# Start slices of the last three pieces of w_out: 28, 36 and 44 for pieces 5, 6 and 7, where only pieces 6 and 7 had start slices, 34 and 44

## The chip, the cores and the metric

The kernel runs on one core of one Trainium2 chip. The metric is the device time of one execution in microseconds (us). Before the change the median of three runs is 434.64 us (432.01 to 434.95).

## What is computed

Three layers follow one another. The first is a decayed linear attention over 2 x 768 tokens with 8 heads of 64. The second, which is where the change lies, projects to 1024 channels, takes the positive part, convolves three neighbouring tokens, gates with a sigmoid and projects back to 512. The third routes each token to one of eight experts and applies that expert's two matrices.

```python
h = np.maximum(x @ w_in, 0.0)                 # 512 -> 1024
conv_out += conv_w[k] * hp[:, k:k + S, :]     # k = 0, 1, 2
gate = 1.0 / (1.0 + np.exp(-conv_out))
x2 = (h * gate) @ w_out                       # 1024 -> 512
logits = x2 @ w_gate; e = argmax(logits)      # with a local gate that may keep the last expert
out = p[e] * (relu(x2 @ w1[e]) @ w2[e])
```

## The kernel before, in words

The inputs w_in and w_out arrive as 64-bit words that hold a float32 each, split over two 32-bit halves. A piece is 128 x 512 numbers. `convert` (line 160) turns one piece into a pair of float32r tiles (high and low part), which the matmuls use as three products (`mm3`, line 131: lines 133, 134, 135). There are 8 pieces of w_in and then 8 of w_out, numbered m = 0 to 7 here.

The steps of `convert` for a piece of w_out are: DMA of the words into `raw` (line 143); `narrow`, which on DVE shifts and merges the high words into `na` (lines 149, 150), on ACT scales the low words in place (line 151) and on POOL adds the two (line 153); then ACT writes the high part `woh` (line 174), DVE the low part `wol` (line 176); PE transposes the piece into `wt_ps` (line 185), ACT copies it out to `wt` (line 189), PE multiplies it by the router's weights into `wc_ps` (line 193), and ACT copies the 9 columns to `wc` (line 195). A `yield n` in these generators says after how many ticks of `advance` (line 404) the next step is issued; so the steps of a piece are spread over the program between other work.

The same engines at the same time run the middle layer for batch 0. `ffn_in` (line 366) takes a block of 128 channels (m = 0 to 7) in 8 slices of 3 matmuls each (`h_ps`, 128 x 384, two halves of the tokens, four slices for each half); ACT takes the positive part (line 376). When a block's slices are over, `hidden` (line 346) follows behind the next block at the ticks of TIMES (line 380): ACT scales by the first tap (line 350), DVE adds the other two (line 353 twice), ACT takes the sigmoid (line 355), DVE multiplies (line 357), ACT cuts off the high part (line 326), DVE the low part (line 330), and PE forms the router's logits `lg` (line 344). So in a block's round of 8 slices each engine has its `hidden` steps at fixed places.

The program is scheduled by hand: each engine executes its instructions in the order in which this Python code issues them. An instruction whose input is late holds everything behind it on its engine. PSUM tiles come from pools: `h_ps` and `wc_ps` share the three buffers of `psa` (line 457) once the attention is over, `wt_ps` has the two of `psg` (line 458). From then on the loop of line 461 issues one slice of `ffn_in` and one `advance` in turn, and `slices[0]` counts the slices.

What sets where a piece begins is the waiting loops ahead of its `narrow`: not more than two other pieces may hold buffers (line 167), and, for pieces named in GATES (line 157), the slice counter must have reached the number given there (line 169).

Of the kernel before, what the change touches and what calls it, by code (L numbers as in the profile page):

```python
# [91 lines left out]
def tile_kernel(ctx, tc, cat, cst, qT, kT, kN, vN, w_in, conv_w, w_out, wg, w1, w2, out):  # L92
# [61 lines left out]
        yield 2  # L154
        return a.bitcast(F32)

    GATES, slices = {6: 34, 7: 44}, [0]
    turning, held, loaded, ready, banks = [], [], [], [], [0]

    def convert(src, hi, lo, m=None):  # L160
# [902 lines left out]
```

## Time and profile before

| what | value |
|---|---|
| median of three runs | 434.64 us (432.01 to 434.95) |
| the profiled execution | 432.95 us, its span 431.2 us |
| PE busy | 408.8 us, 95% of the span |
| DVE, ACT, POOL busy | 289.6, 259.2 and 91.5 us |
| mean granted clock | 0.99 of full speed |

Times in the views are counted from the start of the span. A line of a timeline gives the start, the duration, the engine, the line of the kernel, the operation, the tile written and the tiles read, and in brackets how long the engine was idle before it and what ended that. PE is the matmul engine, and its weight loads, named PEld, run beside it. In the span the middle layer's slices of batch 0 run from about 55 to 135 us, and the attention before and beside them until about 90 us.

### The profile page before, as it was taken

To read this page: it belongs to the slowest core of one execution; us is meant where nothing else is said; L and a number is where in the kernel's file an instruction comes from. 1 tells how busy PE (TensorE), PEld (TensorE's weight loads), DVE (VectorE), ACT (ScalarE), POOL (GpSimd) and SP (SyncE) were. 2 spreads that over 40 slices of the span, in tenths; PEclk is the share of its full clock that TensorE was granted. 3 is DMA by queue.
4 is the path that set the end of the run, shared out by engine and by line. 5 is a ranking of instruction groups with operands and counts; after the bars stand their busy time and mean duration, and the time that the engine had idled before them with its cause. 6 is when DMAs were issued, how large, how long until landed. Compare 5 with 4: busy or idle time off the path is not lost.

```text
span 431.2 us, 7291 instructions
## 1 busy us (share of the span) xinstructions
PE 408.8 (95%) x2412; PEld 329.2 (76%) x2412; DVE 289.6 (67%) x518; ACT 259.2 (60%) x429; POOL 91.5 (21%) x92
## 2 busy tenths in 40 slices
PE   8898999999899999999999999999999999999991
PEld 7787897899798778988768776867738677776880
DVE  3798789787767260377899058968664796858650
ACT  2787677667666212566704166869556686958560
POOL 5256664211110000000000330305203132211210
PEclk9999999999899999999999999999999999999997
DMA  7989763230000101000197899999969999774100
GB/s 229 388 291 398 260 211 92 93 97 1 2 0 2 49 26 49 26 0 2 58 377 254 304 373 379 342 390 409 398 254 340 407 364 346 280 260 186 44 25 29
DMA packets 27324, 86.59 MB, mean 201 GB/s; under 512 B 3598, under 2 KB 4622, under 8 KB 27280
## 3 DMA queue, kind: packets, MB, share of 16 engines
q1 hardware_dynamic: 25200, 79.76, 50.4%
q0 software_dynamic: 2080, 6.29, 3.9%
q8 instruction: 21, 0.34, 0.3%
q14 instruction: 23, 0.19, 0.1%
HBM read 105.18 MB, written 6.55 MB: 259 GB/s over the span
## 4 chain that ended last, share of the span: by engine, by line
PE 35%; issue 26%; DMA 15%; DVE 14%; ACT 4%; POOL 3%; SPq 1%; POOLq 0%; DVEq 0%; ACTq 0%
DMA out_dram<-yo,it 13%; PE h_ps L133 5%; PE h_ps L134 4%; PE h_ps L135 4%; PE x_ps L133 4%; PE x_ps L134 3%; PE x_ps L135 3%; PE y L300 3%; DVE cc L353 3%; PE s_ps L282 2%; POOL xg L727 2%; PE inc L290 1%; DMA kq<-in_qT_dram 1%; PE y L302 1%; DVE na L149 1%
## 5 line engine op out<-in xcount | busy, mean ns | idle before, releaser
L133 PE MATMUL h_ps<-xT,wih 128*128 128x384 f32 x128 | 46.9, 366 | 0.0
L353 DVE SCALAR_TENSOR_TENSOR cc<-h,cw,cc 128x768 f32<-128x768 f32 x32 | 34.4, 1075 | 18.6 <-ACT cc L350 18.5
L863 POOL DMA_INDIRECT out_dram<-yo,it x13 | 16.7, 1282 | 136.3 <-ACT yo L862 136.3
L727 POOL DMA_INDIRECT xg<-xs,it x13 | 18.8, 1444 | 123.4 <-DMA qc<-in_w_dram 115.8
L134 PE MATMUL h_ps<-xT,wih 128*128 128x384 f32 x128 | 43.5, 340 | 0.0
L135 PE MATMUL h_ps<-xT,wil 128*128 128x384 f32 x128 | 43.4, 339 | 0.0
L133 PE MATMUL x_ps<-woh,hg 128*128 128x512 f32 x96 | 38.5, 401 | 0.0
L134 PE MATMUL x_ps<-wol,hg 128*128 128x512 f32 x96 | 37.6, 391 | 0.0
L135 PE MATMUL x_ps<-woh,hg 128*128 128x512 f32 x96 | 37.5, 391 | 0.0
L718 DVE TENSOR_TENSOR ws0l<-r,ws0l 128x1024 fp32r<-128x1024 f32 x22 | 26.0, 1221 | 16.3 <-ACT ws0l L717 16.2
L153 POOL TENSOR_TENSOR na<-na,raw 128x512 int32<-128x512 int32 (+1 forms) x17 | 21.9, 1289 | 48.9 <-ACT raw L151 17.7
L300 PE MATMUL y<-at,vz 128*128 128x128 f32 x192 | 30.6, 281 | 1.8 <-ACT vz L277 0.9
L718 DVE TENSOR_TENSOR ws0h<-r,ws0h 128x1024 fp32r<-128x1024 f32 x22 | 26.0, 1221 | 8.2 <-ACT ws0h L717 8.2
L718 DVE TENSOR_TENSOR wc<-r,wc 128x1024 fp32r<-128x1024 f32 x22 | 25.9, 1221 | 8.0 <-ACT wc L717 8.0
L717 ACT ACTIVATE ws0l<-r 128x1024 fp32r<-128x1024 f32 x22 | 22.1, 1052 | 13.9 <-PE y L135 13.9
L282 PE MATMUL s_ps<-qz,kq 128*128 128x256 f32 x96 | 29.2, 386 | 1.0 <-issue 1.0
L718 DVE TENSOR_TENSOR ws1h<-r,ws1h 128x1024 fp32r<-128x1024 f32 x22 | 26.0, 1221 | 6.0 <-ACT ws1h L717 3.8
L717 ACT ACTIVATE wc<-r 128x1024 fp32r<-128x1024 f32 x22 | 22.1, 1054 | 11.3 <-PE g L135 11.3
L300 PEld LDWEIGHTS y<-at,vz 128*128 128x128 f32 x192 | 25.4, 191 | 4.3 <-DVE xT L305 2.3
L284 DVE TENSOR_TENSOR at<-s_ps,ca 128x256 f32<-128x256 f32 x48 | 20.2, 420 | 11.7 <-PE s_ps L282 11.6
L133 PEld LDWEIGHTS h_ps<-xT,wih 128*128 128x128 f32 x128 | 24.6, 192 | 3.1 <-issue 1.8
L489 ACT ACTIVATE xn<-x_ps 128x512 f32<-128x512 f32 x10 | 6.0, 599 | 32.8 <-PE x_ps L135 18.2
(231 smaller groups left out, 1044.9 us busy)
## 6 DMA issues: line engine op xcount, KB each, us to landing
r<-in_w_dram SPq DMA_DIRECT2D x88, 512.0 KB
qc<-in_w_dram SPq DMA_DIRECT2D x32, 512.0 KB
qs1l<-in_w_dram SPq DMA_DIRECT2D x32, 512.0 KB
raw<-in_w_in_dram SPq DMA_DIRECT2D x8, 512.0 KB
raw<-in_w_out_dram SPq DMA_DIRECT2D x8, 512.0 KB
kq<-in_qT_dram SPq DMA_DIRECT2D x7, 384.0 KB
kq<-in_kT_dram SPq DMA_DIRECT2D x7, 384.0 KB
kv<-in_vN_dram SPq DMA_DIRECT2D x7, 384.0 KB
```

What stands on the lines that cost most here:

```text
L133: te.matmul(ps, lhi, rhi, start=first, stop=False)
L134: te.matmul(ps, lhi, rlo, start=False, stop=False)
L135: te.matmul(ps, llo, rhi, start=False, stop=last)
L153: po.tensor_tensor(out=a, in0=a, in1=lo, op=ALU.add)
L282: te.matmul(ps, self.kq[:, 0, tok], self.qz[:, :, tok], start=True, stop=True)
L284: ve.tensor_tensor(out=self.at[c], in0=ps, in1=self.dm, op=ALU.mult)
L300: te.matmul(y, vz[:, c, j, :], at[:, j, :], start=(j == 0), stop=(c == 0 and j == 1))
L353: ve.scalar_tensor_tensor(out=cc, in0=h[:, i:i + S], scalar=cw[:, m, i:i + 1], in1=cc, op0=ALU.mult, op1=ALU.add)
L717: se.activation(out=w[:, 0, h, :], in_=r, func=AF.Copy)
L718: ve.tensor_tensor(out=w[:, 1, h, :], in0=r, in1=w[:, 0, h, :].bitcast(F32), op=ALU.subtract)
L727: return po.indirect_dma_start(out=xg, out_offset=None, in_=xs[0:n], in_offset=bass.IndirectOffsetOnAxis(ap=it[:, j:j + 1], axis=0), bound ...
L863: po.indirect_dma_start(out=out, out_offset=bass.IndirectOffsetOnAxis(ap=it[:, j:j + 1], axis=0), in_=yo, in_offset=None, bounds_check=NT ...
```

## The change

GATES gets an entry for piece 5 and a later one for piece 6. Blocks have 8 slices, so 28, 36 and 44 are the same place (the middle) in the rounds of three blocks in a row.

```diff
-    GATES, slices = {6: 34, 7: 44}, [0]
+    GATES, slices = {5: 28, 6: 36, 7: 44}, [0]
```

No instruction is added or taken away. PE, DVE and ACT get another order in about three rounds; SP (which issues the loads) and POOL keep theirs. In the rows below a number behind a name tells buffers apart (na_1196 before and na_1232 after are both piece 5, na_1295 and na_1306 piece 6, na_1373 piece 7; cc_1285 before and cc_1279 after are the same block's channels, and so are cc_1218 and cc_1214). A semaphore that the instruction waits for stands in brackets.

ACT, in the first round after slice 28, before:

```order
L195 ACTIVATE wc_96<-wc_ps_1248 128x9 [waits PE_49]
L376 ACTIVATE h0_131<-h_ps_1238 128x384 [waits PE_49]
L195 ACTIVATE wc_96<-wc_ps_1257 128x9
L350 ACTIVATE cc_1285<-h0_131,cw_93 128x768 [waits Activation_49]
L189 ACTIVATE wt_1287<-wt_ps_1262 128x512
L189 ACTIVATE wt_1293<-wt_ps_1276 128x512 [waits PE_49]
L151 ACTIVATE raw_1134<-raw_1134 128x512 [waits DMAHW1_49]
L376 ACTIVATE h1_132<-h_ps_1281 128x384 [waits PE_49]
L326 ACTIVATE hg_1307<-cc_1218 128x768 [waits DVE_49]
L355 ACTIVATE cc_1285<-cc_1285 128x768 [waits DVE_49]
```

ACT at the same place, now:

```order
L195 ACTIVATE wc_96<-wc_ps_1245 128x9 [waits PE_49]
L376 ACTIVATE h0_131<-h_ps_1236 128x384 [waits PE_49]
L195 ACTIVATE wc_96<-wc_ps_1255 128x9
L174 ACTIVATE woh_102<-na_1232 128x512 [waits Pool_49]
L350 ACTIVATE cc_1279<-h0_131,cw_93 128x768 [waits Activation_49]
L189 ACTIVATE wt_1281<-wt_ps_1260 128x512
L376 ACTIVATE h1_132<-h_ps_1275 128x384 [waits PE_49]
L326 ACTIVATE hg_1301<-cc_1214 128x768 [waits DVE_49]
L189 ACTIVATE wt_1304<-wt_ps_1288 128x512
L151 ACTIVATE raw_1134<-raw_1134 128x512 [waits DMAHW1_49]
```

The scaling of the next block (line 350, cc_1285 and cc_1279) stood straight behind two small copies; now the high part of piece 5 (line 174, na_1232), which waits for POOL, stands ahead of it. Before, that instruction (as na_1196) stood seven rows ahead of line 350.

DVE in the same round, before:

```order
L353 SCALAR_TENSOR_TENSOR cc_1218<-h2_133,cw_93,cc_1218 128x768 [waits DVE_49]
L176 TENSOR_TENSOR wol_103<-na_1196,woh_102 128x512 [waits Activation_49]
L330 TENSOR_TENSOR hg_1235<-cc_1108,hg_1235 128x768 [waits Activation_49]
L353 SCALAR_TENSOR_TENSOR cc_1285<-h0_131,cw_93,cc_1285 128x768 [waits PE_49,Activation_49]
L149 TENSOR_SCALAR na_1295<-raw_1134 128x512 [waits DMAHW1_49,PE_49]
L150 SCALAR_TENSOR_TENSOR na_1295<-raw_1134,na_1295 128x512 [waits DVE_49]
L357 TENSOR_TENSOR cc_1218<-cc_1218,h2_133 128x768
```

and now:

```order
L353 SCALAR_TENSOR_TENSOR cc_1214<-h2_133,cw_93,cc_1214 128x768 [waits DVE_49]
L149 TENSOR_SCALAR na_1232<-raw_1083 128x512 [waits DMAHW0_49,PE_49]
L150 SCALAR_TENSOR_TENSOR na_1232<-raw_1083,na_1232 128x512 [waits DVE_49]
L330 TENSOR_TENSOR hg_1229<-cc_1108,hg_1229 128x768 [waits Activation_49]
L353 SCALAR_TENSOR_TENSOR cc_1279<-h0_131,cw_93,cc_1279 128x768 [waits PE_49,Activation_49]
L176 TENSOR_TENSOR wol_103<-na_1232,woh_102 128x512 [waits Pool_49]
```

The two `narrow` steps of a piece (lines 149, 150) stood behind the first tap of the next block (line 353); now they stand ahead of it and ahead of line 330. Those of piece 5 had stood four rows above the first one shown. The same pattern follows one round later with piece 6; piece 7 keeps its two rows where they were.

PE in the round of piece 7 (block after slice 44), before:

```order
L133 MATMUL h_ps_1399<-xT_159,wih_100 128x384
L134 MATMUL h_ps_1399<-xT_159,wih_100 128x384
L135 MATMUL h_ps_1399<-xT_159,wil_101 128x384
L193 MATMUL wc_ps_1409<-wgs_92,wt_1364 128x9 [waits Activation_49]
L193 MATMUL wc_ps_1409<-wgs_92,wt_1364 128x9 x3
L185 MATMUL wt_ps_1415<-cs_91,na_1373 128x128 [waits Pool_49]
L185 MATMUL wt_ps_1415<-cs_91,na_1373 128x128 x3
L133 MATMUL h_ps_1399<-xT_197,wih_100 128x384
```

and now:

```order
L133 MATMUL h_ps_1399<-xT_159,wih_100 128x384
L134 MATMUL h_ps_1399<-xT_159,wih_100 128x384
L135 MATMUL h_ps_1399<-xT_159,wil_101 128x384
L185 MATMUL wt_ps_1410<-cs_91,na_1373 128x128 [waits Pool_49]
L185 MATMUL wt_ps_1410<-cs_91,na_1373 128x128 x3
L133 MATMUL h_ps_1399<-xT_197,wih_100 128x384
L134 MATMUL h_ps_1399<-xT_197,wih_100 128x384
L135 MATMUL h_ps_1399<-xT_197,wil_101 128x384
L193 MATMUL wc_ps_1419<-wgs_92,wt_1371 128x9 [waits Activation_49]
L193 MATMUL wc_ps_1419<-wgs_92,wt_1371 128x9 x3
```

The transposes of piece 7 (line 185), which wait for POOL, stood behind the router product of piece 6 (line 193); now they stand ahead of it, with three matmuls between. The rounds of pieces 5 and 6 have their transposes at the same place, after the first half's second slice.

## Rows read from the trace of the kernel before

**Rows 1.** Page, parts 1 and 2: busy us (share), and PE's granted clock
```profile
PE 408.8 (95%) x2412; PEld 329.2 (76%) x2412; DVE 289.6 (67%) x518; ACT 259.2 (60%) x429; POOL 91.5 (21%) x92
PEclk9999999999899999999999999999999999999997
```
**Rows 2.** Waits of PE, 60 to 250 us: total, times, longest
```profile
PE wc_ps L193 <- ACT h L376: 1.6, 1, 1.6
PE pb L621 <- DVE pi L558: 0.8, 1, 0.8
```
**Rows 3.** Windows: us, then busy us (instructions) by engine, PEclk, DMA share, GB/s
```profile
110.00:111.00 1.00, 0.00 (x0) 0.00 (x0) 0.55 (x1) 1.00 (x3) 0.00 (x0) 1.00 0.00 0
...
114.00:115.00 1.00, 1.00 (x5) 1.00 (x4) 1.00 (x2) 0.44 (x1) 0.00 (x0) 0.50 0.00 0
```
**Rows 4.** Timeline of PE, 100 to 123 us
```profile
100.52 0.95 PE L193 MATMUL wc_ps<-wgs,wt 128*128 128x9 f32 x8
101.33 0.63 PE L185 MATMUL wt_ps<-cs,na 128*128 128x128 f32 x4
101.72 0.42 PE L133 MATMUL h_ps<-xT,wih 128*128 128x384 f32 x1
...
103.42 0.44 PE L133 MATMUL h_ps<-xT,wih 128*128 128x384 f32 x1
...
109.60 0.34 PE L135 MATMUL h_ps<-xT,wil 128*128 128x384 f32 x1
111.50 1.35 PE L193 MATMUL wc_ps<-wgs,wt 128*128 128x9 f32 x8 [1.57 <-ACT h L376]
...
113.46 0.67 PE L133 MATMUL h_ps<-xT,wih 128*128 128x384 f32 x1
...
116.06 0.34 PE L133 MATMUL h_ps<-xT,wih 128*128 128x384 f32 x1
...
122.19 0.34 PE L133 MATMUL h_ps<-xT,wih 128*128 128x384 f32 x1
```
**Rows 5.** Timeline of POOL, 90 to 120 us
```profile
97.63 1.32 POOL L153 TENSOR_TENSOR na<-na,raw 128x512 int32<-128x512 int32 x1 [4.62 <-ACT wt L189]
107.09 1.76 POOL L153 TENSOR_TENSOR na<-na,raw 128x512 int32<-128x512 int32 x1 [8.13 <-DVE na L150]
```
**Rows 6.** Timeline of DVE, 95 to 132 us
```profile
102.34 0.69 DVE L176 TENSOR_TENSOR wol<-na,woh 128x512 fp32r<-128x512 f32 x1
102.94 0.95 DVE L330 TENSOR_TENSOR hg<-cc,hg 128x768 fp32r<-128x768 f32 x1
104.75 1.02 DVE L353 SCALAR_TENSOR_TENSOR cc<-h,cw,cc 128x768 f32<-128x768 f32 x1 [0.86 <-ACT cc L350]
105.69 0.42 DVE L149 TENSOR_SCALAR na<-raw 128x512 int32<-128x512 int32 x1
106.14 0.69 DVE L150 SCALAR_TENSOR_TENSOR na<-raw,na 128x512 int32<-128x512 int32 x1
106.75 0.95 DVE L357 TENSOR_TENSOR cc<-cc,h 128x768 f32<-128x768 f32 x1
107.62 2.05 DVE L353 SCALAR_TENSOR_TENSOR cc<-h,cw,cc 128x768 f32<-128x768 f32 x1
```
**Rows 7.** Timeline of ACT, 95 to 132 us
```profile
95.61 0.59 ACT L189 ACTIVATE wt<-wt_ps 128x512 f32<-128x512 f32 x1
...
98.03 0.94 ACT L350 ACTIVATE cc<-h,cw 128x768 f32<-128x768 f32 x1
98.99 0.63 ACT L174 ACTIVATE woh<-na 128x512 fp32r<-128x512 f32 x1
...
103.21 0.16 ACT L195 ACTIVATE wc<-wc_ps 128x9 f32<-128x9 f32 x1
103.26 0.48 ACT L376 ACTIVATE h<-h_ps 128x384 f32<-128x384 f32 x1
...
103.78 0.94 ACT L350 ACTIVATE cc<-h,cw 128x768 f32<-128x768 f32 x1
...
120.21 0.92 ACT L350 ACTIVATE cc<-h,cw 128x768 f32<-128x768 f32 x1
```

## The prediction

> **What bounds the kernel now.** The page first: PE is busy for 95% of the span, and its granted clock is at full speed (2.4 GHz) but for one slice of the forty and the tail [rows 1]. So PE sets the pace, and time is won or lost where PE stands still or runs slowly. The waits of PE from 60 to 250 us come next: the longest is 1.6 us, a router product of line 193 that waits for ACT's line 376; the second is half as long [rows 2]. The windows place it: from 110 to 111 us PE does nothing, and from 114 to 115 us the granted clock is 0.50, which is 1.2 GHz [rows 3]. PE had been busy up to the hole, the hole came first, and the low clock followed.
>
> The timeline of PE prices that place [rows 4]. The last matmul ahead of the hole starts at 109.60; the next would have followed after 0.17 us (twelve matmuls of 128 x 384 take 2.06 us start to start), at 109.77, and starts at 111.50: 1.73 us lost. At full clock a router product and the transposes behind it last 101.72 - 100.52 = 1.20 us; here they last 113.46 - 111.50 = 1.96 us. The nine matmuls behind them last 116.06 - 113.46 = 2.60 us against 9 x 0.172 = 1.55 us. The clock costs 0.76 + 1.05 = 1.81 us, the whole place 3.5 us. That is 0.8% of the time and the most that a better place for the pieces can win here; from 116.06 to 122.19 PE runs without a hole to speak of.
>
> Why ACT was late is in the timelines of DVE and POOL. POOL's addition for piece 6 (line 153) runs from 107.09 to 108.85 [rows 5]; it takes 1.76 us where the one for piece 5 took 1.32. DVE's line 353, issued at 107.62, takes 2.05 us where the same instruction took 1.02 at 104.75 [rows 6]. Each held the other: the addition waited for line 357, which ended at 107.70, and line 353 waited for the addition. From 107.70 to 108.85 is 1.15 us: an addition ends 1.15 us after the DVE instruction that held it.
>
> **What the change does, step by step.** No instruction comes or goes, and SP's and POOL's order stays, so no load moves past another in a queue. Three pieces get the same place in three rounds. I walk the new order with durations of before; an instruction of ACT or DVE that waits for nothing starts about 0.08 us before its predecessor's recorded end [rows 6].
>
> Round one. ACT's copy at 95.61 is common to both orders [rows 7]. Line 151 of piece 5 no longer stands behind it, so the next block's line 350 starts at 95.61 + 0.49 + 0.39 + 0.49 + 0.53 = 97.51 instead of 98.03: ACT's steps for line 189, line 376, line 189 again and line 174, start to start. The early part gains 0.5 us. DVE follows: line 353 at 97.51 + 0.97 = 98.48, then line 176 (+0.94), 357 (+0.60), 353 (+0.87), 149 (+0.94), 150 (+0.45), which gives 102.28, and line 330 (+0.61) at 102.89, to 103.84. Line 150 ends at 102.97, and POOL would start 0.26 us later (106.83 to 107.09 in [rows 5, 6]); but line 330 is then running, as line 357 was in [rows 6], so the addition ends at 103.84 + 1.15 = 104.99. ACT meanwhile reaches the row that the change put ahead of line 350: line 174, which needs that sum. ACT is there at 103.7 (before, line 350 started there, at 103.78 [rows 7]) and waits 1.3 us. PE starts the block at 103.29 instead of 103.42 (the copy of line 195, which frees its buffer, ends at 103.24 by the walk and ended at 103.37 [rows 7]); its six matmuls last 6 x 0.172 + 0.12 = 1.15 us, it reaches the transposes at 104.44, and they wait for the sum: 0.6 us of hole, up to 105.05.
>
> From here it is a ring, the same in all three rounds: line 174 on ACT, line 350, then DVE's 353, 176, 357, 353, 149, 150 and 330, POOL's addition held until 330 ends, and line 174 of the next piece. Its length, start to start: 0.53 + 0.97 + 0.94 + 0.60 + 0.87 + 0.94 + 0.45 + 0.61 + 0.95 + 1.15 + 0.04 = 8.05 us, from [rows 6, 7] and the 1.15 above. PE's own work between two sets of transposes is one block: 24 matmuls at 0.172, logits 0.46, router product 0.81, transposes 0.39, and 0.65 of starts behind changes of shape: 6.44 us. So PE stands still for 8.05 - 6.44 = 1.6 us in each round. The second set of transposes starts at 105.05 + 8.05 = 113.10, the third at 121.15. Behind the third come three matmuls (0.39 + 0.64 us), the router product (0.81) and three more (0.63): the next block starts at 121.15 + 2.47 = 123.6. In the trace of before it starts at 122.19 [rows 4]. **The sum is +1.4 us.** It holds the hole and the low clock of before, which go, and three new holes (0.6, 1.6 and 1.6 us), which come.
>
> What is late next: ACT's line 350 of the following block, at about 121.7 against 120.21 [rows 7]. No piece is left in the rounds behind it, DVE and ACT get by on less than PE's 5.8 us for each, and the logits still find their input ready, by half a microsecond. The lag of PE stays and is carried to the end, since PE's later waits are 0.8 us at most up to 250 us [rows 2].
>
> The profiled execution took 432.95 us (span 431.2 and 1.75 around it), so the sum gives 434.4 on its own base. The three timed runs have a median 1.7 us higher, and what is forecast is a median: 434.64 + 1.4 = 436.0 us.
>
> One price has two bounds: whether line 330 holds POOL. The rows show line 357 holding it (1.76 against 1.32 us, [rows 5]), and both are the same operation, with both inputs in SBUF. If 330 does not hold it, the addition ends 0.26 + 1.28 after line 150, at 104.5, and the ring is 0.49 us shorter: three rounds give 1.4 us back and the sum is zero. I take the held value, because the row nearest to it is the same operation on the same engine.
> The Trainium skill has two pages on this. "Advanced Engine Details and Errata", section "VectorE Performance Modes", names only Vector instructions in a two-port mode as blocking GpSimd, and gives tensor_tensor no such mode; by it the sum would be zero. "SBUF — State Buffer", section "Who interferes with whom", says that a Vector instruction with two inputs in SBUF contends with a GpSimd instruction that reads SBUF, and that the first to issue holds the other for its whole length; by it the sum is +1.4. This case's trace agrees with the second, with its 1.76 us addition and its 2.05 us line 353.
>
> **The rivals.** (1) The third hole lowers the clock as the hole of before did (1.73 us there, 1.6 here). A fall behind the second hole costs 1.8 us too, but the third hole takes 1.6 of it; one behind the third is paid in full: 1.4 + 1.8 = +3.2, 437.8 us. For it speaks the equal size, against it that a hole of 0.6 us and PE's many short gaps lowered nothing. (2) Line 330 does not hold POOL: 434.6 us, as worked out. (3) Faster: evenly spaced pieces never meet the stream, the hole of 109.77 goes and nothing comes for it: 434.64 - 3.5 = 431.1 us. It needs a ring of no more than 6.44 us, or the sum ready when ACT reaches line 174, 1.3 us earlier than the walk has it; that line 330 stands between line 150 and the addition speaks against it. (4) Slower: the clock stays at 1.2 GHz from the second hole to the end of the third round. PE's 6.44 + 2.47 = 8.9 us of work would take 2.60 / 1.55 = 1.68 times as long, 15.0 us from 113.1: the next block starts at 128.1, 5.9 us later than before, 440.5 us. It decides from some 11 us of low clock on, since each costs 0.4 us and the third hole absorbs 1.6; before, the clock was low for about 4 us.
>
> **How the numbers follow.** Sum as worked out, with or without a low clock that the third hole absorbs: 0.53. Rival 1: 0.23. Rival 2: 0.10. Rival 3: 0.07. Rival 4: 0.07. The predicted time is 436.0 us. The range leaves out rivals 3 and 4 (0.14): below it takes rival 2 less half the spread of the runs shown (434.6 - 1.5 = 433.1), above rival 1 with 0.8 us for its clock, 438.6. About 1% of the time, 4.3 us, is what a measurement of this kernel can tell from no change. Faster by more than that would need more than the 3.5 us that the place holds: 0.03. Slower by more than that is rival 4 with a little of rival 1: 0.09. Within 1%: 0.88.
>
> **What would show it.** Line 350 of the three rounds in the timeline of ACT, 8 us apart (about 97.5, 105.6, 113.7, 121.7), each straight behind a line 174 that waited for POOL; PE's transposes of line 185 waiting for POOL three times, 0.6, 1.6 and 1.6 us; additions of about 1.8 us; the block behind the third set at about 123.6 us. The hole at 109.8 us gone, with its wait for line 376. Wrong would be: additions of 1.3 us (rival 2), line 350 less than 7 us apart and no wait at line 185 (rival 3), or a granted clock of 0.5 in the stretch around 121 to 125 us (rival 1) or throughout from 113 us on (rival 4).

## The result, and the profile after

The changed kernel takes 436.93 us in the median of 11 runs (435.09 to 438.70), the kernel before 434.64 us in 11 runs beside it. The ratio is 1.0053, with a 95% interval of 1.0028 to 1.0078, which is 2.3 us more, from 1.2 to 3.4. The forecast was 436.0 us, a sum of +1.4.

| what | before | after |
|---|---|---|
| median | 434.64 us | 436.93 us |
| profiled execution, its span | 432.95, 431.2 us | 436.16, 434.4 us |
| mean granted clock of that execution | 0.990 | 0.988 |
| PE's waits for POOL at line 185, 60 to 250 us | none among those listed | 3.4 us in 3 |
| PE's wait for line 376 at line 193 | 1.6 us | none |

The page of the changed kernel, the row of PE in part 1 and the granted clock in part 2, answers [rows 1]:

```profile
PE 407.4 (94%) x2412; PEld 328.0 (76%) x2412; DVE 288.2 (66%) x518; ACT 258.8 (60%) x429; POOL 92.2 (21%) x92
PEclk9999999999999999999999899999999999999996
```

The low slice of before, the eleventh (108 to 119 us), is full now. Another has fallen in its stead, the twenty-third, at about 245 us. The waits of PE from 60 to 250 us (total, times, longest) answer [rows 2]:

```profile
PE wt_ps L185 <- POOL na L153: 3.4, 3, 1.6
PE tp L813 <- DMA xg<-xs,it: 2.3, 1, 2.3
```

The hole at line 193 is gone and three at line 185 have come, all behind POOL's additions. The second row, a transpose of gathered tokens far behind the change, was 0.8 us before. The timeline of ACT (start, duration, line, tiles, idle time ahead) shows the instruction that makes the ring:

```profile
104.35 0.63 ACT L174 ACTIVATE woh<-na 128x512 fp32r<-128x512 f32 x1 [1.37 <-POOL na L153]
104.89 0.92 ACT L350 ACTIVATE cc<-h,cw 128x768 f32<-128x768 f32 x1
...
112.36 0.63 ACT L174 ACTIVATE woh<-na 128x512 fp32r<-128x512 f32 x1 [0.97 <-POOL na L153]
112.90 0.92 ACT L350 ACTIVATE cc<-h,cw 128x768 f32<-128x768 f32 x1
...
120.37 0.63 ACT L174 ACTIVATE woh<-na 128x512 fp32r<-128x512 f32 x1 [0.92 <-POOL na L153]
120.91 0.92 ACT L350 ACTIVATE cc<-h,cw 128x768 f32<-128x768 f32 x1
```

Three times line 350 stands straight behind a line 174 that waited for POOL, 8.01 us apart. The timelines of DVE and POOL show the link from line 330 to the addition (the first round):

```profile
102.21 0.95 DVE L330 TENSOR_TENSOR hg<-cc,hg 128x768 fp32r<-128x768 f32 x1
105.84 1.02 DVE L353 SCALAR_TENSOR_TENSOR cc<-h,cw,cc 128x768 f32<-128x768 f32 x1 [2.68 <-ACT cc L350]
```
```profile
102.55 1.77 POOL L153 TENSOR_TENSOR na<-na,raw 128x512 int32<-128x512 int32 x1 [10.16 <-ACT wc L195]
110.58 1.75 POOL L153 TENSOR_TENSOR na<-na,raw 128x512 int32<-128x512 int32 x1 [6.26 <-DVE na L150]
118.56 1.77 POOL L153 TENSOR_TENSOR na<-na,raw 128x512 int32<-128x512 int32 x1 [6.24 <-ACT raw L151]
```

The addition ends at 104.32, 1.16 us after line 330 (103.16), and lasts 1.77 us. DVE then stands idle for 2.68 us because line 350 is late, and that delay comes back to POOL one round later. And the timeline of PE, the end of the third round, for the block whose start was forecast:

```profile
120.39 0.66 PE L185 MATMUL wt_ps<-cs,na 128*128 128x128 f32 x4 [1.61 <-POOL na L153]
...
122.83 0.34 PE L133 MATMUL h_ps<-xT,wih 128*128 128x384 f32 x1
```

That block starts 0.64 us later than at 122.19 in [rows 4], although this execution left the attention 0.63 us earlier: its first logits (line 344) start at 94.76, those of before at 95.39. Over the rounds it lost 1.27 us.

For the comparisons below, **the stretch** is the time on PE from the first line-344 group after 94 us to the sixth: 34.71 us before (95.39 to 130.10) and 35.99 us after (94.76 to 130.75). The difference of 1.28 us is made up as follows. Before holds a hole of 1.57 and a low clock of 1.81. After holds holes of 0.27, 0.46, 0.18, 1.33 and 1.61, together 3.85. That leaves 31.33 against 32.14 us, or 0.8 us for the same instructions. In the new order three matmuls stand between line 185 and line 193 in each round, so PE changes shape more often; that this is what costs was read from the order and not tried by itself. Most of the remainder is not the holes' doing: the first experiment, with one hole of 0.28 us and the same three matmuls between, keeps 32.12 - 0.28 = 31.84 us, 0.5 us more than before.

### The profile page after: what moved, and what is told of

The parts are those of the page before. It is cut to its first block, busy times and chain, and to the rows that moved or that the text cites. A ratio compares the mean times of both kernels' runs of the same rounds, so it can differ in the third digit from the quotient of the medians.

```text
span 434.4 us, 7289 instructions
## 1 busy us (share of the span) xinstructions
PE 407.4 (94%) x2412; PEld 328.0 (76%) x2412; DVE 288.2 (66%) x518; ACT 258.8 (60%) x429; POOL 92.2 (21%) x92
## 4 chain that ended last, share of the span: by engine, by line
PE 32%; issue 27%; DMA 17%; DVE 14%; ACT 4%; POOL 3%; SPq 1%; POOLq 0%; DVEq 0%; ACTq 0%
DMA out_dram<-yo,it 15%; PE h_ps L133 4%; PE x_ps L133 4%; PE h_ps L134 4%; PE h_ps L135 4%; PE x_ps L134 3%; PE x_ps L135 3%; PE y L300 3%; DVE cc L353 3%; PE s_ps L282 2%; DMA kv<-in_kN_dram 2%; PE inc L290 1%; DVE na L150 1%; DVE cc L357 1%; PE y L302 1%
## 5 line engine op out<-in xcount | busy, mean ns | idle before, releaser
L353 DVE SCALAR_TENSOR_TENSOR cc<-h,cw,cc 128x768 f32<-128x768 f32 x32 | 33.3, 1042 | 23.0 <-ACT cc L350 22.9
L489 ACT ACTIVATE xn<-x_ps 128x512 f32<-128x512 f32 x10 | 6.0, 599 | 32.8 <-PE x_ps L135 15.5
```

What stands on the lines that cost most here:

```text
L353: ve.scalar_tensor_tensor(out=cc, in0=h[:, i:i + S], scalar=cw[:, m, i:i + 1], in1=cc, op0=ALU.mult, op1=ALU.add)
```

## The experiments

**One step later, the ring is open.** The edit puts a tick of delay between the narrowing of a late piece and its line 174. That instruction then stands behind line 350 on ACT and no longer ahead of it; what follows in the piece (line 176 on DVE, the transposes of line 185 on PE) comes a tick later too.

```diff
         w = yield from narrow(words, 512)
+        if m in GATES: yield 1
```

> Edit on the changed kernel: pieces of w_out issue line 174 and all their steps behind it one tick later, so that ACT's line 350 stands ahead of line 174. Ring theory (ACT waits at line 174 for POOL's sum, which waits for line 330, and line 350 stands behind it, 8.05 us a round): the ring is open, line 350 comes about 6.4 us after its predecessor (DVE's own rounds with one held addition), the three waits of line 185 for POOL go, the place of the three rounds gets some 4 us shorter: about 431.5 us, ratio to before 0.990 to 0.995. Rival A (the time is lost at the gather behind the second layer, where PE waited 2.3 us for line 727 in the changed kernel against 0.8 before, because the later rounds shift it against the loads): the rounds get shorter but the time stays near 436 us. Rival B (DVE and POOL together are the bound of a round, whatever the order on ACT): line 350 stays 7.5 to 8 us apart, 435 to 437 us.

Measured: 430.84 us against 434.07 us for before, ratio 0.991 (0.9877 to 0.9943). ACT's timeline and the window from 110 to 130 us (busy time of PE, PEld, DVE, ACT, POOL, then the clock):

```profile
109.40 0.94 ACT L350 ACTIVATE cc<-h,cw 128x768 f32<-128x768 f32 x1
110.77 0.63 ACT L174 ACTIVATE woh<-na 128x512 fp32r<-128x512 f32 x1 [0.36 <-POOL na L153]
115.80 0.94 ACT L350 ACTIVATE cc<-h,cw 128x768 f32<-128x768 f32 x1
```
```profile
110.00:130.00 20.00, 20.00 (x140) 17.89 (x139) 15.51 (x20) 13.95 (x25) 3.04 (x3) 1.00 0.00 1
```

Line 350 comes every 6.15 to 6.40 us, PE is busy for all 20 us, and the stretch is 32.12 us. The slices are the same 28, 36 and 44, and the additions are as long as in the changed kernel (1.78, 1.81 and 1.78 us). So neither the place in the round nor the held addition costs the time by itself: the wait of line 174 ahead of line 350 sets the 8 us. The transposes, which are no link of that ring, now stand behind nine matmuls of the block and not six, and start 0.06 us after each sum is ready (the additions end at 104.40, 110.73 and 117.05, the transposes start at 104.46, 110.79 and 117.11). How much of the three holes went by this later place, and how much by the shorter round, was not parted. The time is 3.2 us below before, where rival 3 priced 3.5. This version beats both kernels.

**Two slices later.** The same opening without an added step (against the changed kernel):

```diff
-    GATES, slices = {5: 28, 6: 36, 7: 44}, [0]
+    GATES, slices = {5: 30, 6: 38, 7: 46}, [0]
```

> Edit on the changed kernel: GATES = {5: 30, 6: 38, 7: 46}, the same place in each round again, but two slices later; line 174 then stands behind line 350 on ACT and lines 149 and 150 behind line 330 on DVE, with no other edit. Ring theory: what costs is that line 174 stands ahead of line 350 and the transposes ahead of the sum, not that the pieces have the same place: the ring is open, lines 350 about 6.4 us apart, no wait of line 185 for POOL, the stretch of logits near 32.2 us, time as with the extra tick, about 431 us, ratio 0.990 to 0.995. Rival (three pieces in three consecutive rounds are too dense for DVE and POOL wherever they stand): lines 350 7.5 to 8 us apart, ratio 1.000 to 1.005.

Measured: 431.49 against 433.72 us, ratio 0.9957 (0.9931 to 0.9982). Line 350 comes 6.33, 6.61 and 6.78 us apart, PE's waits at line 185 are 0.5 us in two, and the stretch is 32.80, all a little more than expected (ratio 0.990 to 0.995, 32.2 us). Here POOL issues first, and then it is DVE that is held (POOL's timeline, then DVE's):

```profile
103.62 1.31 POOL L153 TENSOR_TENSOR na<-na,raw 128x512 int32<-128x512 int32 x1 [11.11 <-DVE na L150]
```
```profile
104.25 1.50 DVE L353 SCALAR_TENSOR_TENSOR cc<-h,cw,cc 128x768 f32<-128x768 f32 x1 [0.88 <-ACT cc L350]
```

**One slice earlier** ({5: 27, 6: 35, 7: 43} in the same line).

> Edit on the changed kernel: GATES = {5: 27, 6: 35, 7: 43}, the same place in each round, one slice earlier. Line 174 still stands ahead of line 350 on ACT, but lines 149 and 150 now stand ahead of DVE's second line 353 instead of behind it. Ring theory: the ring stays closed but is shorter: line 350 to 353 0.97, then 0.94, 0.87 (line 357), 0.45, 0.61, line 353 held against the addition 1.01, addition 1.15, 0.04, line 174 0.53, line 376 0.39: 6.96 us a round against 8.05. Lines 350 come 7.0 us apart, the stretch from the first to the sixth group of logits is about 3 us shorter than the 36.0 of the changed kernel, 432 to 433.5 us, ratio to before 0.995 to 0.999: between the changed kernel and the two with the ring open. Rival (only the order of lines 174 and 350 counts, so a closed ring costs what it cost in the changed kernel): lines 350 8 us apart, ratio 1.005.

Measured: 432.34 against 435.49 us, ratio 0.9947 (0.9914 to 0.9979), a little better than expected. Line 350 is 7.68, 7.09 and 7.08 us apart against an expected ring of 6.96, the additions are held (1.82 to 1.85 us), PE waits 0.8 us in two at line 185 and 0.96 us once for line 195, the clock does not fall, and the stretch is 33.77 (about 33 was expected). ACT's timeline shows that line 174 still waits ahead of line 350:

```profile
110.83 0.63 ACT L174 ACTIVATE woh<-na 128x512 fp32r<-128x512 f32 x1 [0.31 <-POOL na L153]
111.37 0.47 ACT L376 ACTIVATE h<-h_ps 128x384 f32<-128x384 f32 x1
111.87 0.94 ACT L350 ACTIVATE cc<-h,cw 128x768 f32<-128x768 f32 x1
```

The ring is shorter, and so are the holes.

**The held addition by itself.** The ticks of lines 326 and 330 are moved in three blocks (11 and 13 become 13 and 14), so that line 330 comes later and POOL goes first; the slices stay those of the change.

```diff
-    LATE = {(B - 1, 5): ...
+    LATE = {**{(0, m): (0, 1, 3, 4, 10, 13, 14, 15) for m in (1, 2, 3)}, (B - 1, 5): ...
```

> Edit on the changed kernel: for blocks 1 to 3 of batch 0 line 326 goes from tick 11 to 13 and line 330 from 13 to 14, so that line 330 becomes ready only after POOL's addition has begun. Ring theory with line 330 as a link: the additions last 1.3 us instead of 1.76, the ring is 0.49 us shorter (7.55 us between lines 350), the third transposes come 1.5 us earlier: about 1.5 us less than the changed kernel, ratio to before about 1.001. Rival (the addition is slow for another reason, such as ACT's or PE's traffic): additions stay at 1.76 us, line 350 stays 8.0 us apart, time as the changed kernel, ratio about 1.005.

Measured: 432.77 against 434.07 us, ratio 0.9974 (0.9946 to 1.0001). POOL's and ACT's timelines:

```profile
111.82 1.28 POOL L153 TENSOR_TENSOR na<-na,raw 128x512 int32<-128x512 int32 x1 [6.27 <-DVE na L150]
119.34 1.28 POOL L153 TENSOR_TENSOR na<-na,raw 128x512 int32<-128x512 int32 x1 [6.24 <-DVE na L150]
```
```profile
106.12 0.92 ACT L350 ACTIVATE cc<-h,cw 128x768 f32<-128x768 f32 x1
...
113.14 0.63 ACT L174 ACTIVATE woh<-na 128x512 fp32r<-128x512 f32 x1 [0.65 <-POOL na L153]
113.67 0.92 ACT L350 ACTIVATE cc<-h,cw 128x768 f32<-128x768 f32 x1
```

The ring still closes (line 174 waits ahead of line 350), but a round is 7.52 to 7.59 us, not 8.01: that is the 0.49 us by which the prediction shortened it without the hold. The stretch is 34.55 us, 1.4 less than the changed kernel's, as rival 2 worked out for three rounds. The time is a miss: the expected ratio of about 1.001 lies outside the interval, and the median is some 1.6 us lower than expected. The ring accounts for the 1.4 us only. The mean granted clock of these twelve executions is higher too (median 0.9925 against 0.987), but whether that is the rest is not shown.

**One piece of the change at a time.** First piece 5 alone ({5: 28, 6: 34, 7: 44}), then piece 6 alone ({6: 36, 7: 44}).

> One part alone: GATES = {5: 28, 6: 34, 7: 44}, so only piece 5 is moved. Ring theory by the walk: round one as in the changed kernel (line 350 1.7 us later than before, a hole of 0.6 us at line 185), then piece 6 meets the stream as before, with line 353 held by the addition, and PE waits for line 376 again, some 2 us: 1.7 us slower than before, ratio 1.004. Rival (the moves add up evenly, 1.15 us of the measured 2.3 each): ratio 1.0026.

> One part alone: GATES = {6: 36, 7: 44}, so only piece 6 is moved and piece 5 begins as early as before. Ring theory by the walk: round one as before without piece 6 in it (line 350 at 103.8), rounds two and three 8.05 us each, holes of 1.0 and 1.6 us at line 185, the hole before line 193 gone: the block behind the third transposes starts at 121.9 against 122.2 before, 0.3 us faster than before without a low clock, ratio 0.999. Rival (the moves add up evenly): ratio 1.0026.

Piece 5 alone: 434.04 us, ratio 0.9975 (0.9944 to 1.0007). That is a miss: 1.004 lies outside. The stretch is 35.07 us, 0.4 over the 34.71. The walk had kept the hole of before at line 193 and its low clock behind the new hole; the trace has no low clock there and only a rest of the hole. PE itself was later (among others 1.3 us in a wait of line 344 for line 357); line 376 ends at 113.36 us, and line 193 starts at 113.42, some 0.3 us later than it could. Piece 6 alone: 434.04 us, ratio 0.9997 (0.9963 to 1.0031), the time as expected, but with one wait of 2.1 us at line 185 where two of 1.0 and 1.6 were worked out, and a stretch of 33.68 us. The prices of the two pieces, +0.4 and -1.0 us in the stretch, don't add up to the +1.28 of both. Each version alone already has a round of the ring's length (8.06 us between lines 350 with piece 5, 8.02 with piece 6), and each takes away the hole and the low clock of before, 3.4 us that can be won only once. How the rest divides was not tried.

**The same kernels once more.** A single pair of profiles can't tell how often the clock falls, so before and the changed kernel were each profiled again, unchanged.

> The kernel before, unchanged, profiled once more. The walk's sum took the low clock behind the hole of line 193 (1.81 us) as part of before. Theory C (a hole of this size lowers the clock in some executions and not in others): the hole of 1.5 to 1.8 us ahead of line 193 is there again with the same wait for line 376, and the granted clock behind it may stay at 1.00; then the stretch from the first to the sixth group of logits behind 95 us (34.7 us in the first profile) takes 33.0 us. Rival (the hole always lowers it): 34.7 us again, granted clock near 0.5 for some 3 us behind the hole.

> As the run ahead of it, a third profile of the kernel before: 33.0 us or 34.7 us between the first and the sixth group of logits behind 95 us, by whether the granted clock falls behind the hole.

> The changed kernel, unchanged, profiled once more. Ring theory: lines 350 8.0 us apart again, three waits of line 185 for POOL. Theory C: the clock may fall behind one of the holes; if it falls behind the third, the stretch between the first and the sixth group of logits takes 36.0 + 1.8 = 37.8 us, otherwise 36.0 to 36.4 us. The wait of line 813 for the gather at about 245 us, 2.3 us in the first profile of after and 0.8 in that of before, comes out anywhere between 0.7 and 3 us if it has nothing to do with the change, and at 2 us or more if the change causes it.

> The changed kernel, profiled a third time, for two terms that the walk left to chance. Clock: it fell behind a hole in three of three profiles of before and in one of two of the changed kernel; the stretch of logits is 36.0 us without a fall and 37.3 us or more with one. Gather: if the change makes the wait of line 813 longer, it is 1.0 us or more again (0.5 to 0.8 in three profiles of before); if not, it is 0.5 to 0.8 in some of these.

> As the run ahead of it, a fourth profile of the changed kernel: stretch of logits 36.0 or 37.3 us and more; wait of line 813 1.0 us or more if the change causes it.

| execution | span | stretch | clock, 110 to 130 us | wait at line 813 |
|---|---|---|---|---|
| before, as shown | 431.2 | 34.71 | 0.91 | 0.8 |
| before, second | 431.6 | 36.26 | 0.83 | 0.5 |
| before, third | 432.2 | 34.68 | 0.91 | 0.6 |
| after, as shown | 434.4 | 35.99 | 1.00 | 2.3 |
| after, second | 433.1 | 37.28 | 0.83 | 1.0 |
| after, third | 431.1 | 36.01 | 1.00 | none listed |
| after, fourth | 432.5 | 37.33 | 0.83 | 1.6 |

The windows of the second and the third execution of the changed kernel, one after the other:

```profile
110.00:130.00 20.00, 18.66 (x110) 17.21 (x110) 12.49 (x16) 12.20 (x23) 3.58 (x3) 0.83 0.00 1
...
113.00:114.00 1.00, 1.00 (x6) 1.00 (x6) 0.00 (x0) 1.00 (x2) 0.00 (x0) 0.50 0.00 0
```
```profile
110.00:130.00 20.00, 17.06 (x117) 15.32 (x117) 12.96 (x17) 12.52 (x24) 4.05 (x3) 1.00 0.00 0
```

Up to the second hole the two run alike: line 350 is 8.07 and 8.02 us apart in the one, 8.07 and 8.01 in the other, and the hole itself is 1.34 and 1.32 us. Behind it the clock is at 0.50 (1.2 GHz) in the one and stays at 2.4 GHz in the other. Where it fell, the third hole is gone, since PE came later than the sum, and the stretch is 1.3 us longer. The three executions of before all have the hole at line 193 with a low clock behind it, worth 1.8 us twice and 3.4 us once (20 x 0.09 and 20 x 0.17). The means of the stretch are 35.22 us (before, three) and 36.65 us (after, four): +1.43. The means of these spans are 431.7 and 432.8 us, 1.1 apart.

## Why the prediction was right

**The ring, and what it costs.** The steps stand beside the rows, with 0.63 us added to the times measured, by which that execution came earlier out of the attention.

| step | forecast | measured |
|---|---|---|
| first line 350 | 97.5 | 96.82 + 0.63 = 97.45 |
| ring, start to start | 8.05 | 8.07, 8.01, 8.01 |
| waits at line 185 | 0.6, 1.6, 1.6 | 0.46, 1.33, 1.61 |
| POOL's additions | 1.76 | 1.77, 1.75, 1.77 |
| the block behind the third set | 123.6 | 122.83 + 0.63 = 123.46 |

The ring came out to 0.04 us, and the experiments show that it is the cause of the long rounds: with the ring open, the same three slices cost nothing, and with rings of 8.01, 7.55 and 7.08 us the stretch is 36.0, 34.55 and 33.77 us, against 32.1 and 32.8 with the ring open. The second hole is 0.27 us shorter than forecast, because PE lost 0.18 us waiting for line 357 and had more breaks between shapes in that round.

**The addition held by line 330.** This was the price with two bounds, and the held value was right: 1.75 to 1.77 us here, 1.28 to 1.31 us where line 330 or 353 does not come first. The Trainium skill's "SBUF — State Buffer", section "Who interferes with whom", says that the first to issue keeps the other out. The rows agree in both directions: line 330 lengthens the addition by some 0.5 us, and in the kernel with slices 30, 38 and 46 the addition lengthens line 353 from 1.02 to between 1.50 and 1.60 us.

**The rivals.** Rival 2 fell with the additions, rival 3 with the waits at line 185, and rival 4 with the windows: the clock came back before the third round was over. Rival 1 is the one that was partly true. In two of the four profiled executions the clock fell, not behind the third hole but behind the second. That case had been priced at 1.8 - 1.6 = 0.2 us; it costs 1.3. The step that was too small is the length of the low clock: 20 x 0.17 = 3.4 us where the 1.81 us of before had been carried over. Less the third hole's 1.6 us, that leaves 1.8, of which the stretch shows 1.3. One of the three executions of before has such a longer fall as well, so that the means of the stretch differ by the sum's own +1.4 is in part luck.

**The rest, from +1.4 to +2.3 us.** The interval (1.2 to 3.4) holds the forecast, so there need be no rest. If there is one, the clock is the likeliest place: the sum counts before's 1.81 us of low clock as won, and on the average it is not won. The mean granted clock of the 11 executions of the changed kernel lies from 0.983 to 0.991, median 0.987; that of 29 of before (those beside the first experiment) from 0.980 to 0.992, median 0.987 too. The one execution of the changed kernel without a fall from 95 to 250 us has 0.996. Span times mean clock, a rough measure of what a full clock would have taken, has a median of 427.2 us in the 29 of before and of 429.3 us in the 11 of after: +2.1 us. Holes of 3.85 for 1.57 us bring in 2.3, and the 0.8 us of the new order would make it 3.1, so the match is rough. That the clock fell in the unprofiled executions behind these holes is not shown, since only the mean is recorded there.

**The 3.2 us between the two spans shown** are not the change's price. 0.64 us are the lag behind the rounds and 1.5 us the longer wait at line 813. Behind that wait the clock is low, and from one group of line 813 to the next it is 3.35 us where before it was 1.86, another 1.5 us; 0.4 us are given back between there and the end. PE's timeline before, then after:

```profile
244.82 1.13 PE L813 MATMUL tp<-cs,xg 128*128 128x128 f32 x8 [0.79 <-DMA xg<-xs,it]
246.68 1.06 PE L813 MATMUL tp<-cs,xg 128*128 128x128 f32 x8
```
```profile
246.93 2.04 PE L813 MATMUL tp<-cs,xg 128*128 128x128 f32 x8 [2.30 <-DMA xg<-xs,it]
250.28 1.06 PE L813 MATMUL tp<-cs,xg 128*128 128x128 f32 x8
```

The windows of the changed kernel:

```profile
205.00:250.00 45.00, 41.39 (x218) 33.16 (x217) 30.57 (x90) 15.09 (x21) 4.44 (x6) 0.96 0.68 247
```
```profile
247.00:248.00 1.00, 1.00 (x5) 1.00 (x6) 0.00 (x0) 0.00 (x0) 0.00 (x0) 0.50 0.65 141
```

That wait varies between executions of one and the same kernel, from 2.3 us to none listed. Some 18 us ahead of it ACT waits for a write of tokens, here in the timeline of the changed kernel as shown and in its third execution:

```profile
228.94 0.60 ACT L489 ACTIVATE xn<-x_ps 128x512 f32<-128x512 f32 x1 [9.68 <-DMA xs<-xn]
```
```profile
227.43 0.60 ACT L489 ACTIVATE xn<-x_ps 128x512 f32<-128x512 f32 x1 [8.04 <-DMA xs<-xn]
```

In the seven executions the two longest waits at line 813 (2.3 and 1.6 us) go with the two longest of ACT (9.68 and 9.25 us); that the one causes the other is not shown. The three of before have 0.5 to 0.8 us at line 813, the four of after 0 to 2.3. Whether the change shifts its mean stays open.

## What to carry to other kernels

Before an instruction is moved ahead of another on an in-order engine, follow what it waits for: if that chain leads back to the instruction that is now behind it, the round takes the length of the chain, however little each engine has to do. Add up that ring with held durations and compare it with the bounding engine's own work in a round; here 8.05 against 6.44 us told the holes to about 0.3 us, and one step of delay opened the ring. Work that comes at even distances is no help if it comes at the wrong place in each round.

## What the runs showed of the hardware

- **The clock falls behind some holes and not behind others of the same length.** Behind the changed kernel's second hole (1.32 to 1.34 us) it fell in two of four executions, behind its third (1.6 us) in neither of the two that had it, behind the 1.57 us of before in three of three, behind the 2.1 us of piece 6 alone not at all (1.00 from 110 to 130 us). So a row can't say what one hole will cost, only that behind some of them another 1.8 to 3.4 us went.
- **Most of what the open ring wins is clock.** Its six executions have a median clock of 0.995 against 0.987, which is 3.4 us of 429; its span times clock is 426.9 us, next to the 427.2 of before. The version two slices later says the same: 0.9935 against 0.987, and 426.7 against 427.0 us. Span times clock is the rough measure named above, so the share is no more exact than that.
